# Second step of a long convolution: products taken from an SBUF copy of both halves, and one accumulator buffer for two quarters of the last step

## The chip, the cores and the metric

The kernel runs on one core of a Trainium2 chip. TensorE (PE) multiplies matrices into PSUM, an accumulator memory of eight banks; VectorE (DVE), ScalarE (ACT) and GpSimd (POOL) work elementwise; SyncE (SP) issues most of the DMAs. The metric is device time in microseconds (us) of one execution, as the median of several runs. Lower is better.

## The reference

Two branches over 2048 positions of 640 channels are mixed by a gate. Branch a is a long convolution whose filter comes from a state-space model of 128 modes per channel; branch b is a feed-forward network (FFN) with 1728 hidden units and a relu.

```python
g = sigmoid((x * gate_w).sum(-1, keepdims=True))        # x = A_u, [1, 2048, 640]
# branch a
dt = exp(log_dt); A = -exp(log_A_real) + 1j * A_imag; C = (C_real + 1j * C_imag) * dt[:, None]
P = exp((A * dt[:, None])[:, :, None] * arange(2048))   # [640, 128, 2048]
K = 2.0 * einsum("dn,dnl->dl", C, P).real
a = irfft(rfft(u^T, 4096) * rfft(K, 4096), 4096)[..., :2048]^T + u * D_skip
# branch b
b = maximum(x @ w1, 0) @ w2                             # w1 [640, 1728], w2 [1728, 640]
return g * a + (1 - g) * b
```

## The kernel before

**Three pieces of work.** `ssm` makes the filter K (up to about 404 us of the profile), `conv` convolves (from about 407 us to the end), `feed_forward` computes the FFN. The FFN's matmuls run all through the execution and take turns with the other two. Its 14 blocks of hidden units are handled in three parts (`PARTS`); partial sums of a part go to DRAM and come back for the next.

**The convolution.** `conv` takes the channels in five column groups of 128 (index `i`). A group passes through steps, each a set of small matmuls with an operation on another engine behind it:

- `stage1` (first step): four quarters of the filter and four of the signal are transformed; VectorE transposes the results into a buffer `ku` of 128 x 8 x 2 x 512, whose halves are called `K` and `U`. Two such buffers exist.
- `stage2` (second step): for each of eight indices `j`, TensorE writes 128 x 1024 results into one PSUM buffer `pc`: one half belongs to the filter, the other to the signal. Then they are multiplied as complex numbers: ScalarE copies the filter's half to `K`; VectorE makes two products of 128 x 512 (`mul(1)` first, into `U`, then `mul(0)`, into `K` in place), each reading the signal's half from PSUM and the filter's from SBUF; GpSimd combines them with one subtraction and one addition of 128 x 256 (`add`).
- `inv2` (next step): two halves `h` of four indices each. Each half takes two `pc` buffers, and ScalarE copies them back to `U` (128 x 1024 each). It needs the `add` results of its four indices.
- `relay`: eight VectorE transposes from `U` to `K`.
- `inv1` (last step): four quarters. TensorE writes 128 x 512 of a quarter into a `pc` buffer, of which half is used; ScalarE scales it by the gate in four instructions. Then the result is stored, or added to the FFN's sums and written out.

`pc` buffers come from a pool `psc` of three, each two PSUM banks. The FFN has two single banks of its own (`pf`). In the profile the second step's matmuls are `pc<-ku,tm`, those of `inv2` are `pc<-ku,tn`, those of `inv1` are `pc<-ku,tw`, and those of the first step are `pc<-ck,tf`, `pc<-cl,tf` and `pc<-xu,tf`.

**The order of the work.** No engine chooses at run time. A planner (`Plan.run`) lays out the whole kernel in advance: every operation is a task with an engine, a queue, an expected duration, its dependencies, a rank, and tokens of buffer rings (`take` when it begins to hold a buffer, `use` as long as it holds it). The instructions of an engine then stand in the order so found and wait for their operands by semaphores. FFN matmuls have rank 5, those of the second step and `inv2` rank 2, those of `inv1` rank 3. A task of VectorE marked `port` is planned longer when GpSimd is busy beside it:

```python
if t.port:                                                                     # L286
    self.free[e] += 0.25 * min(max(self.free['POOL'] - start, 0), t.dur)       # L288
```

The planner gives a product of the second step 0.62 us and each add 0.7 us. Most instructions are issued through one helper, so most rows of the profile carry its line, L314, and are told apart by the names of their tiles.

Of the kernel before, what the change touches and what calls it, by code (L numbers as in the profile page):

```python
# [10 lines left out]
F32 = mybir.dt.float32  # L11
# [14 lines left out]
S4R = 3  # L26
# [27 lines left out]
S2D = 1  # L54
# [5 lines left out]
PL = 2.5  # L60
YO = 5
YJ = 3
KRANK = 3
TN = 0.7

# [76 lines left out]
class Plan:  # L142
# [20 lines left out]
    def add(self, eng, q, dur, fn, deps=(), take=(), use=(), rank=5, mode=None, kb=0, port=False, n=0, late=False):  # L163
        t = Task()
        t.eng, t.q, t.dur, t.fn, t.deps, t.take, t.use, t.mode = eng, q, dur, fn, tuple(deps), take, use, mode
        t.prio, t.end, t.kb, t.lag, t.glue, t.port = rank + MOVES.get(self.n, 0), None, kb, self.LAG[eng], [], port
        t.n, t.late = n or dur / 0.13, late
        self.n += 1
        for b in (*take, *use):
            b.users += 1  # L170
            b.left += 1
        if q is not None:
            self.put(t, q)
        return t
# [170 lines left out]
class Kernel:  # L345
# [865 lines left out]
    def conv(self, C=128):  # L1211
        tc, nc, io, A, tok, ring = self.tc, self.nc, self.io, self.plan.add, self.plan.token, self.plan.ring
        V, S, P, D_ = self.V, self.S, self.P, self.D
        n, H = D // C, C // 2
        od = self.out.rearrange("(a h b) d -> h a b d", h=2, b=16)
        ud = io['A_u'][0].rearrange("(a b) d -> a b d", b=32)
        for k, v in dict(psc=3, ck=2, ckp=2, cu=1, yo=YO, yj=YJ, K=2).items():
            ring(k, v)
        st = {}

# [46 lines left out]
        K, first, pes = {}, {}, {}  # L1267
# [49 lines left out]
        def stage2(i, j, dep):  # L1317
            b_ = tok('psc')

            def pe():  # L1320
                ps = self.psc.tile([128, 2, 4, C], F32, name="pc")
                for a in range(2):
                    for m in range(4):
                        for p in range(2):
                            r, g = slice(p * 64, p * 64 + 64), 4 * j + m
                            x = st['ku', i].rearrange("p j k (e m t) -> p j m k e t", m=4, t=2)
                            self.E.matmul(ps[32 * m:32 * m + 32, p, 2 * a:2 * a + 2].rearrange("q k (e t) -> q k e t", t=2),
                                          st['tm'][r, g, 32 * a:32 * a + 32], x[r, j, m], start=True, stop=True)
                st['p2', i, j] = ps.rearrange("q p (a k) c -> q k a p c", a=2)

            def copy():
                S.copy(whole(i, j), st['p2', i, j][:, 0])

            def mul(a):
                def go():
                    k = whole(i, j)
                    V.tensor_mul(whole(i, j, 'U') if a else k, st['p2', i, j][:, 1, None, a].to_broadcast([128, 2, 2, C]), k)
                return go

            def add(k):  # L1340
                def go():
                    y, x = whole(i, j)[:, k], whole(i, j, 'U')[:, 1 - k]
                    (P.tensor_add if k else P.tensor_sub)(y, y, x)
                return go
            f = A('PE', None, 0.92, pe, dep, take=[b_], use=[K[i]], rank=S2P, mode='c', n=32)
            c = [A('ACT', 's2', 0.52, copy, [f], use=[b_, K[i]], rank=0.5)]
            for a in (1, 0):
                c.append(A('DVE', 's2', 0.62, mul(a), c, use=[b_, K[i]], rank=S2D))
            return f, [A('POOL', 's2', 0.7, add(k), c, use=[K[i]], rank=1) for k in range(2)]


        def whole(i, j, k='K'):
            return st[k, i][:, j].rearrange("q (b p c) -> q b p c", b=2, p=2)
# [40 lines left out]
        def inv1(i, j, dep):  # L1394
            last = i == n - 1
            for q in range(2):
                b_, b0 = tok('psc'), j * 8 + q * 4
                ns = min(max(2 * sum(c <= i for c in CG) - b0, 0), 4)
                y_ = tok('yo') if ns or not last else None
                g_, first = None, False  # L1400
                if last and ns < 4:
                    first = self.gy_tok is None
                    g_ = self.gy_tok = self.gy_tok or tok('K')

                def pe(q=q, b0=b0):
                    py = st['p4', i, b0] = self.psc.tile([128, 2, 4, C], F32, name="pc")
                    for h in range(2):
                        self.E.matmul(py[h * 64:h * 64 + 64, 0].rearrange("p b c -> p (b c)"), st['tw'],
                                      st['K', i][:, h * 4 + b0 // 4], start=True, stop=True)

                def copy(q=q, b0=b0, ns=ns, y_=y_, first=first):
                    if first:
                        self.gy = self.pr.tile([128, 8, 2, 512], F32, name="ku", bufs=2).rearrange("p j k (b c) -> p (j k b) c", c=C)
                    if y_:
                        st['yo', i, b0] = self.pr.tile([128, 4, C], F32, name="yo", bufs=YO)
                    x = st['p4', i, b0][:, 0].rearrange("p b c -> p (b c)").rearrange("p (c b) -> p b c", b=4)
                    for b in range(4):
                        o = self.gy[:, b0 + b] if last and b >= ns else st['yo', i, b0][:, b]
                        S.mul(o, x[:, b], self.gate[:, b0 + b:b0 + b + 1])
                a = A('PE', 's4', 0.87, pe, [*dep, tw], take=[b_], use=[K[i]], rank=S4R, mode='c1')  # L1420
                pes['4', i, b0] = a
                if JS4 and q:
                    self.plan.join([pes['4', i, b0 - 4], a])
                c = A('ACT', 's4', 1.24, copy, [a], take=[x for x in (y_, g_ if first else None) if x],
                      use=[b_] + ([g_] if g_ and not first else []), rank=S4A)
                self.need_gates.append(c)
                if ns < 4:
                    if not last:
                        def store(b0=b0, ns=ns):
                            stq.dma_start(self.sc['y'][:, b0 + ns:b0 + 4, i * C:i * C + C], st['yo', i, b0][:, ns:])  # L1430
                        c2 = A(STQ, 'y4', 0.62, store, [c], use=[y_], kb=64 * (4 - ns), rank=STR, late=True)
                    self.y_st[i, b0 // 4] = c if last else c2
                if ns:

                    new = not last or b0 == 0
                    if last:
                        j_ = self.yl_tok = tok('cu') if new else self.yl_tok
                    else:
                        j_ = tok('yj')

                    def load(b0=b0, ns=ns):
                        if last:
                            if b0 == 0:
                                st['yl'] = self.xu[:, :16 * C].rearrange(
                                    "p (b c) -> p b c", c=C)
                            st['yj', i, b0] = st['yl'][:, b0:b0 + 4]
                        else:
                            st['yj', i, b0] = self.pr.tile([128, 4, C], F32, name="yj", bufs=YJ)
                        for b in range(0, ns, 2):
                            D_.dma_start(st['yj', i, b0][:, b:b + 2],  # L1450
                                         self.sc['part'][(len(PARTS) - 1) % 2][(b0 + b) // 2][:, :, i * C:i * C + C])

                    def join(b0=b0, ns=ns):
                        y = st['yo', i, b0][:, :ns]
                        P.tensor_add(y, y, st['yj', i, b0][:, :ns])

                    def out(b0=b0, ns=ns):
                        for h in range(2):
                            stq.dma_start(od[h, :, b0:b0 + ns, i * C:i * C + C], st['yo', i, b0][64 * h:64 * h + 64, :ns])
                    ld = A('SP', 'yq', 0.62 * ((ns + 1) // 2), load, [opened], take=[j_] if new else (), use=() if new else [j_],  # L1460
                           kb=64 * ns, rank=3)
                    self.need_sums.append((ld, [(b0 + b) // 2 for b in range(0, ns, 2)]))
                    own = A('POOL', 's4', 0.1 + 0.3 * ns, join, [c, ld], use=[y_, j_], rank=2)
                    A(STQ, 'y4', 1.25, out, [own], use=[y_], kb=64 * ns, rank=STR, late=True)
# [4 lines left out]
        u = load_u(0)  # L1469
# [3 lines left out]
        dep = [x for q in range(4) for x in stage1('k', 0, q, lk[q])]  # L1473
# [67 lines left out]
```

## Time and profile before

| | before |
|---|---|
| median of 3 runs | 644.57 us (643.6 to 645.45) |
| the profiled execution, own time | 642.35 us |
| its span, first to last instruction | 640.6 us |
| TensorE busy | 617.3 us (96%) |
| VectorE busy | 508.5 us (79%) |
| ScalarE busy | 402.1 us (63%) |
| GpSimd busy | 93.9 us (15%) |
| granted TensorE clock | 1.0 |

The profile is one execution recorded by the hardware. A row names the engine, the operation, the tiles written and read, the shapes, how often it ran, its busy time in us and the mean of one in ns, and then how long its engine had been idle just before and what ended that idleness. A view by windows gives the busy time of each engine in stretches of the span. A timeline row has a start, a duration and the idle time before; neighbouring instructions of one kind are merged, with their count. Matmuls overlap, so the duration of one is longer than the distance to the next.

### The profile page before, as it was taken

What the parts mean: (1) busy time and instruction counts of PE and PEld (TensorE: products, weight loads), DVE (VectorE), ACT (ScalarE), POOL (GpSimd) and SP (SyncE); (2) the same over time, 40 slices, a digit from 0 to 9 for tenths busy, and PEclk for the clock granted to TensorE, in tenths of its full rate; (3) what the DMA queues carried; (4) which work ended last, traced back from release to release, by engine and by line L of the source; (5) the groups of instructions that cost most, each with busy time, mean ns of one, the idle gap of its engine ahead of it and who ended that gap; (6) DMA issues with size and microseconds to landing.
All of it is one profiled execution on the core that took longest, in us unless ns stands there. A gap on an engine that the chain in (4) does not pass through costs nothing.

```text
span 640.6 us, 19212 instructions
## 1 busy us (share of the span) xinstructions
PE 617.3 (96%) x8236; PEld 503.0 (79%) x8236; DVE 508.5 (79%) x818; ACT 402.1 (63%) x603; POOL 93.9 (15%) x134
## 2 busy tenths in 40 slices
PE   7989999899999899999999999999999999999897
PEld 6989998798898798898898898665565556756577
DVE  4889936989999999998999999768579753966542
ACT  5557439999999988988978985113443424432550
POOL 0000000000000000000000000024151531713633
PEclk9999999999999999999999999999999999999999
DMA  9974774333456734373454225794406558156355
GB/s 256 326 236 147 221 229 165 105 125 112 136 167 210 255 122 144 122 242 117 129 198 154 79 80 176 258 315 132 144 3 215 185 164 263 53 158 188 102 166 133
DMA packets 76176, 107.78 MB, mean 168 GB/s; under 512 B 7610, under 2 KB 58682, under 8 KB 75195
## 3 DMA queue, kind: packets, MB, share of 16 engines
q1 hardware_dynamic: 75930, 106.14, 53.2%
q8 instruction: 65, 1.06, 0.7%
q10 hardware_dynamic: 160, 0.41, 0.3%
q14 instruction: 21, 0.16, 0.1%
HBM read 67.47 MB, written 44.30 MB: 174 GB/s over the span
## 4 chain that ended last, share of the span: by engine, by line
PE 56%; DVE 5%; DMA 2%; ACT 2%; issue 1%; SPq 1%; DVEq 0%; ACTq 0%
PE pf L314 35%; PE pc L314 13%; PE pk L314 4%; DVE ku L314 3%; PE pg L314 2%; PE px L314 2%; DMA part<-q 1%; ACT ku L314 1%; PE pe L314 1%; DMA out_dram<-yo 1%; SPq L314 1%; DVE sn L314 1%; ACT cs L314 0%; DVE q L314 0%; ACT q L314 0%
## 5 line engine op out<-in xcount | busy, mean ns | idle before, releaser
L314 PE MATMUL pf<-xx,w1h 128*128 128x256 f32 (+1 forms) x760 | 184.2, 339 | 0.4 <-DVE xx L314 0.3
L314 PEld LDWEIGHTS pf<-xx,w1h 128*128 128x128 f32 x760 | 125.2, 189 | 22.8 <-issue 7.3
L314 PE MATMUL pf<-xx,w1l 128*128 128x512 f32 (+1 forms) x340 | 115.7, 340 | 0.0
L314 PE MATMUL pf<-w2h,hh 128*128 128x320 f32 x288 | 89.7, 315 | 2.4 <-DVE hl L314 1.5
L314 PE MATMUL pf<-w2l,hh 128*128 128x320 f32 x288 | 87.8, 309 | 0.0
L314 ACT COPY ku<-pc 128x512 f32<-128x512 f32 (+1 forms) x60 | 43.8, 761 | 68.2 <-PE pc L314 56.7
L314 PE MATMUL pf<-w2h,hl 128*128 128x320 f32 x256 | 73.3, 312 | 0.0
L314 PEld LDWEIGHTS pf<-xx,w1l 128*128 128x128 f32 x340 | 64.3, 189 | 7.6 <-DVE w1l L314 0.2
L314 POOL TENSOR_TENSOR kt<-kt,dsk 128x8 f32<-128x8 f32 x20 | 10.3, 515 | 392.7 <-DVE kt L314 377.8
L314 POOL TENSOR_TENSOR ku<-ku 128x256 f32<-128x256 f32 x80 | 56.2, 737 | 55.3 <-DVE ku L314 49.1
L314 DVE TENSOR_TENSOR ku<-pc,ku 128x512 f32<-128x512 f32 x80 | 52.6, 684 | 12.5 <-ACT ku L314 11.3
L314 DVE STREAM_TRANSPOSE ku<-pc 128x512 f32<-128x512 f32 x80 | 50.2, 683 | 13.7 <-PE pc L314 13.7
L314 PEld LDWEIGHTS pf<-w2h,hh 128*128 128x128 f32 x288 | 54.1, 188 | 7.7 <-issue 3.7
L314 DVE TENSOR_TENSOR sn<-pg,cs 128x1024 f32<-128x1024 f32 x40 | 48.7, 1217 | 7.5 <-ACT cs L314 7.5
L314 PEld LDWEIGHTS pf<-w2l,hh 128*128 128x128 f32 x288 | 54.1, 188 | 0.6
L314 ACT ACT_TABLE_LOAD x42 | 53.9, 1283 | 0.7
L314 ACT CAST cs<-pg 128x1024 int32<-128x1024 f32 x40 | 40.3, 1008 | 21.2 <-PE pg L314 21.0
L314 DVE TENSOR_TENSOR mg<-mg,cs 128x1024 f32<-128x1024 f32 x40 | 48.9, 1222 | 1.3
L314 PEld LDWEIGHTS pf<-w2h,hl 128*128 128x128 f32 x256 | 46.4, 188 | 3.5 <-issue 2.9
L314 PE MATMUL pc<-ku,tm 64*32 64x256 f32 x1280 | 42.2, 392 | 3.6 <-DVE ku L314 2.4
L314 ACT ACTIVATE cs<-cs,half_pi 128x1024 f32<-128x1024 f32 x40 | 45.6, 1140 | 0.0
L314 ACT ACTIVATE hh<-pf 128x512 fp32r<-128x512 f32 (+1 forms) x40 | 20.5, 513 | 39.4 <-PE pf L314 39.4
(170 smaller groups left out, 1232.5 us busy)
## 6 DMA issues: line engine op xcount, KB each, us to landing
xx<-xt SPq DMA_DIRECT2D x24, 640.0 KB, 6.8
xt<-xx SPq DMA_DIRECT2D x16, 640.0 KB, 3.9
part<-q SPq DMA_DIRECT2D x16, 640.0 KB, 3.4
q<-part SPq DMA_DIRECT2D x16, 640.0 KB, 5.3
ws<-in_B_w_dram SPq DMA_DIRECT2D x20, 320.0 KB, 5.5
kd<-kt SPq DMA_DIRECT2D x80, 64.0 KB, 1.8
ub<-in_A_u_dram SPq DMA_DIRECT2D x10, 512.0 KB, 4.7
xu<-ub SPq DMA_DIRECT2D x5, 1024.0 KB, 6.2
```

Source lines behind the costliest of these rows:

```text
L314: self._last = self._tc.keep_in_program_order(f(*a, **k))
```

## The change

All eight indices `j` of the second step are handled in a new way (`FULL`). ScalarE copies both halves of the PSUM buffer, 128 x 1024, to `K` and `U`. The two products read the signal's half from `U` in place of PSUM; `mul(1)` writes into a new SBUF buffer `ut` (two of them, `UT`), and the adds read it from there. In the planner the PSUM buffer's token is no longer held by the products, the products are marked `port`, and the copy is given 0.96 us in place of 0.52. In the last step the two quarters `q` of one `j` use the two halves of one `pc` buffer, in place of a buffer each.

```diff
+FULL = tuple(range(8))
+UT = 2
+FULLR = 0
...
-        for k, v in dict(psc=3, ck=2, ckp=2, cu=1, yo=YO, yj=YJ, K=2).items():
+        for k, v in dict(psc=3, ck=2, ckp=2, cu=1, yo=YO, yj=YJ, K=2, ut=UT).items():
...
+            full = j in FULL
+            t_ = tok('ut') if full else None
+
             def copy():
-                S.copy(whole(i, j), st['p2', i, j][:, 0])
+                if full:
+                    S.copy(st['ku', i][:, j].rearrange("q k (a p c) -> q k a p c", a=2, p=2), st['p2', i, j])
+                else:
+                    S.copy(whole(i, j), st['p2', i, j][:, 0])
 
             def mul(a):
                 def go():
                     k = whole(i, j)
-                    V.tensor_mul(whole(i, j, 'U') if a else k, st['p2', i, j][:, 1, None, a].to_broadcast([128, 2, 2, C]), k)
+                    u = whole(i, j, 'U')[:, a] if full else st['p2', i, j][:, 1, a]
+                    if a:
+                        st['x2', i, j] = whole(i, j, 'U')
+                        if full:
+                            st['x2', i, j] = self.pr.tile([128, 4 * C], F32, name="ut", bufs=UT).rearrange("q (b p c) -> q b p c", b=2, p=2)
+                    V.tensor_mul(st['x2', i, j] if a else k, u[:, None].to_broadcast([128, 2, 2, C]), k)
                 return go
 
             def add(k):
                 def go():
-                    y, x = whole(i, j)[:, k], whole(i, j, 'U')[:, 1 - k]
+                    y, x = whole(i, j)[:, k], st['x2', i, j][:, 1 - k]
                     (P.tensor_add if k else P.tensor_sub)(y, y, x)
                 return go
             f = A('PE', None, 0.92, pe, dep, take=[b_], use=[K[i]], rank=S2P, mode='c', n=32)
-            c = [A('ACT', 's2', 0.52, copy, [f], use=[b_, K[i]], rank=0.5)]
+            c = [A('ACT', 's2', 0.96 if full else 0.52, copy, [f], use=[b_, K[i]], rank=0.5)]
             for a in (1, 0):
-                c.append(A('DVE', 's2', 0.62, mul(a), c, use=[b_, K[i]], rank=S2D))
-            return f, [A('POOL', 's2', 0.7, add(k), c, use=[K[i]], rank=1) for k in range(2)]
+                c.append(A('DVE', 's2', 0.62, mul(a), c, take=[t_] if full and a else (), use=[K[i]] + ([] if full else [b_]), rank=S2D + FULLR * full,
+                           port=full))
+            return f, [A('POOL', 's2', 0.7, add(k), c, use=[K[i]] + ([t_] if full else []), rank=1) for k in range(2)]
...
             for q in range(2):
-                b_, b0 = tok('psc'), j * 8 + q * 4
+                b0 = j * 8 + q * 4
+                b_ = b_ if q else tok('psc')
...
-                    py = st['p4', i, b0] = self.psc.tile([128, 2, 4, C], F32, name="pc")
+                    if not q:
+                        st['p4', i, j] = self.psc.tile([128, 2, 4, C], F32, name="pc")
+                    py = st['p4', i, j]
                     for h in range(2):
-                        self.E.matmul(py[h * 64:h * 64 + 64, 0].rearrange("p b c -> p (b c)"), st['tw'],
+                        self.E.matmul(py[h * 64:h * 64 + 64, q].rearrange("p b c -> p (b c)"), st['tw'],
...
-                a = A('PE', 's4', 0.87, pe, [*dep, tw], take=[b_], use=[K[i]], rank=S4R, mode='c1')
+                a = A('PE', 's4', 0.87, pe, [*dep, tw], take=() if q else [b_], use=[K[i]] + ([b_] if q else []), rank=S4R, mode='c1')
```

More of the change, by code (lines that the diff above doesn't have):

```diff
@@ L1403, in inv1, with pe, copy @@
                     g_ = self.gy_tok = self.gy_tok or tok('K')
-                def pe(q=q, b0=b0):
-                    py = st['p4', i, b0] = self.psc.tile([128, 2, 4, C], F32, name="pc")
+                def pe(q=q, b0=b0, j=j):
+                    if not q:
+                        st['p4', i, j] = self.psc.tile([128, 2, 4, C], F32, name="pc")
+                    py = st['p4', i, j]
                     for h in range(2):
-                        self.E.matmul(py[h * 64:h * 64 + 64, 0].rearrange("p b c -> p (b c)"), st['tw'],
+                        self.E.matmul(py[h * 64:h * 64 + 64, q].rearrange("p b c -> p (b c)"), st['tw'],
                                       st['K', i][:, h * 4 + b0 // 4], start=True, stop=True)
-                def copy(q=q, b0=b0, ns=ns, y_=y_, first=first):
+                def copy(q=q, b0=b0, ns=ns, y_=y_, first=first, j=j):
                     if first:
@@ L1415, in copy @@
                         st['yo', i, b0] = self.pr.tile([128, 4, C], F32, name="yo", bufs=YO)
-                    x = st['p4', i, b0][:, 0].rearrange("p b c -> p (b c)").rearrange("p (c b) -> p b c", b=4)
+                    x = st['p4', i, j][:, q].rearrange("p b c -> p (b c)").rearrange("p (c b) -> p b c", b=4)
                     for b in range(4):
```

## The prediction

> **What bounds the kernel now.** I read first the page's busy shares, then the same count for the stretch from 400 us on, where all the edited code runs, and then what TensorE waited for there.
>
> ```profile
> span 640.6 us, 19212 instructions
> PE 617.3 (96%) x8236; PEld 503.0 (79%) x8236; DVE 508.5 (79%) x818; ACT 402.1 (63%) x603; POOL 93.9 (15%) x134
> ```
> ```profile
> 400.00:640.60 240.60, 231.84 (x3677) 150.96 (x3675) 154.07 (x251) 83.50 (x168) 82.98 (x108) 1.00 0.55 166
> ```
> ```profile
> PE pc L314 <- DVE ku L314: 3.1, 6, 1.7
> PE pc L314 <- ACT ku L314: 1.0, 1, 1.0
> ```
>
> The columns of the second fence are PE, PEld, DVE, ACT and POOL. TensorE is busy for 231.84 of the last 240.60 us at full clock. Only 8.76 us are open, and its waits for the convolution's own engines are 4.1 us of them. So no gain here can be large; a loss can, because TensorE's order is fixed beforehand and a late operand stops everything behind it.
>
> The second look is at the five stretches in which the second step runs, one per column group, from about its first copy to its last add:
>
> ```profile
> 426.30:440.80 14.50, 14.33 (x373) 9.72 (x362) 12.45 (x20) 4.70 (x8) 11.27 (x16) 1.00 0.59 178
> 460.30:474.50 14.20, 14.08 (x328) 9.29 (x315) 13.93 (x23) 5.01 (x9) 11.25 (x16) 1.00 0.01 3
> 501.20:515.60 14.40, 14.09 (x264) 8.90 (x249) 12.03 (x19) 4.81 (x9) 11.30 (x17) 1.00 0.51 150
> 543.50:558.70 15.20, 15.17 (x359) 10.43 (x352) 14.89 (x24) 6.96 (x12) 12.75 (x18) 1.00 0.18 56
> 592.50:602.40 9.90, 7.30 (x87) 3.91 (x86) 7.45 (x12) 5.79 (x15) 9.88 (x15) 1.00 0.28 69
> sum 68.20, PE 64.97 PEld 42.24 DVE 60.74 ACT 27.26 POOL 56.45; mean PE 12.99 PEld 8.45 DVE 12.15 ACT 5.45 POOL 11.29
> ```
>
> Here VectorE (12.15 us of a mean 13.64) and GpSimd (11.29) are both nearly full. They fit into 13.64 us only because they run at the same time. This is what the change touches.
>
> **The change part by part.** The prices of the operations:
>
> ```profile
> L314 POOL TENSOR_TENSOR ku<-ku 128x256 f32<-128x256 f32 x80 | 56.2, 737 | 55.3 <-DVE ku L314 49.1 <-PE pf L314 6.2
> L314 DVE TENSOR_TENSOR ku<-pc,ku 128x512 f32<-128x512 f32 x80 | 52.6, 684 | 12.5 <-ACT ku L314 11.3
> L314 DVE TENSOR_TENSOR cs<-me,cs 128x512 f32<-128x512 f32 x40 | 27.3, 682 | 0.0
> L314 ACT COPY ku<-pc 128x512 f32<-128x512 f32 x40 | 23.3, 593 | 42.7 <-PE pc L314 42.7
> L314 ACT COPY ku<-pc 128x1024 f32<-128x1024 f32 x20 | 20.7, 1095 | 25.5 <-PE pc L314 14.0 <-issue 11.5
> ```
>
> *The copy.* It grows from 128x512 (593 ns) to 128x1024 (1095 ns): 0.50 us, times 40 is 20 us more ScalarE work. ScalarE has 157 us open after 400 us, so this is free but for the first copy of each stage, which makes the stage 0.5 us later. FFN matmuls hide that; uncovered it would be 5 x 0.5 = 2.5 us. What queues behind it is FFN evictions and the next step's copies, each up to 0.5 us later; the two FFN banks cover this.
>
> *The buffer.* It comes free after the copy, not after two products. That ends the 3.1 us of waits for DVE (bounds 0 and the 4.1 us of both rows); I take 3.1. It also lets the eight matmul groups of a stage run in fewer bursts. What a change of pattern costs:
>
> ```profile
> 544.60 0.73 PE L314 MATMUL pf<-xx,w1h 128*128 128x512 f32 x2
> 545.40 0.62 PE L314 MATMUL pf<-xx,w1h 128*128 128x512 f32 x2
> 546.09 0.61 PE L314 MATMUL pf<-xx,w1h 128*128 128x512 f32 x2
> 546.54 0.39 PE L314 MATMUL pf<-xx,w1l 128*128 128x512 f32 x1
> 546.86 3.26 PE L314 MATMUL pc<-ku,tm 64*32 64x256 f32 x96
> ```
>
> Nine FFN matmuls take 2.26 us (544.60 to 546.86). The middle three took 0.69 (545.40 to 546.09), so 2.07 would do: some 0.2 us per round trip. The second step comes in 18 bursts in TensorE's timeline, of which these are the first and the last:
>
> ```profile
> 425.06 2.99 PE L314 MATMUL pc<-ku,tm 64*32 64x256 f32 x96
> ...
> 596.37 1.16 PE L314 MATMUL pc<-ku,tm 64*32 64x256 f32 x32 [0.50 <-DVE ku L314]
> ```
>
> With two bursts per stage it would be 10, so 8 fewer.
>
> *The shared buffer of the last step.* Its two quarters go into the two halves of one buffer, four quarters into two buffers. Now the last one or two of the four come apart from the others in four of the five stages, for want of a third or fourth buffer; I take 3 round trips less. If the second quarter's matmuls had to wait for the first quarter's four copies, it would cost up to 1.2 us ten times; different halves give no reason for that, so zero. Together 11 round trips x 0.2 = 2.2. Gain: 3.1 + 2.2 = **5.3 us**.
>
> *The products.* They now read two SBUF operands. Alone that costs nothing: 682 ns for the SBUF form, 684 for the present one. [...]
>
> *Products against adds.* GpSimd's adds read two SBUF operands too. The trace of before has such a meeting only in the filter stage, where GpSimd adds 128x8:
>
> ```profile
> L314 POOL TENSOR_TENSOR kt<-kt,dsk x20: 209/568/572, 121.0 to 404.2; 128x8 f32<-128x8 f32 x20
> ```
> ```profile
> 138.51 0.65 DVE L314 SCALAR_TENSOR_TENSOR G<-mg,sn 128x512 f32<-128x512 f32 x1
> 139.09 0.69 DVE L314 TENSOR_TENSOR G<-mg,sn 128x512 f32<-128x512 f32 x1
> ```
> ```profile
> 138.67 0.57 POOL L314 TENSOR_TENSOR kt<-kt,dsk 128x8 f32<-128x8 f32 x1 [17.42 <-DVE kt L314]
> 404.23 0.21 POOL L314 TENSOR_TENSOR kt<-kt,dsk 128x8 f32<-128x8 f32 x1 [11.11 <-DVE kt L314]
> ```
>
> The add takes 0.21 us when VectorE is idle and 0.57 when it meets a VectorE instruction with two SBUF operands: it ends at 139.24, 0.08 after that instruction (139.16). GpSimd waited for its end, though 0.13 of its own 0.21 ran underneath. The present products meet the adds without that: the 80 adds lie within 721 and 757 ns. How far a product waits for an add no row shows. Bounds per group of two products and two adds: 1.4 (GpSimd's two adds, as now) and 2 x 0.65 + 2 x 0.70 = 2.7 us. I take strict alternation with 0.13 hidden at each of four turns, 2.7 - 0.52 = 2.2 us, as the kt row has it. [...]
>
> *What that does to TensorE.* The order is laid out with the products stretched by a quarter of the overlap (line 288), about 1.55 us a group. At 2.2, the eight groups end 8 x 0.65 = 5.2 us later than the order allows for. The next step's second half then waits, less the slack that stands there now:
>
> ```profile
> 439.31 1.42 POOL L314 TENSOR_TENSOR ku<-ku 128x256 f32<-128x256 f32 x2 [0.21 <-DVE ku L314]
> 471.62 2.82 POOL L314 TENSOR_TENSOR ku<-ku 128x256 f32<-128x256 f32 x4 [0.95 <-PE pf L314]
> 507.18 8.36 POOL L314 TENSOR_TENSOR ku<-ku 128x256 f32<-128x256 f32 x12 [0.21 <-DVE ku L314]
> 557.24 1.44 POOL L314 TENSOR_TENSOR ku<-ku 128x256 f32<-128x256 f32 x2 [0.38 <-DVE ku L314]
> 591.28 11.11 POOL L314 TENSOR_TENSOR ku<-ku 128x256 f32<-128x256 f32 x16
> ```
> ```profile
> 453.58 2.09 PE L314 MATMUL pc<-ku,tn 32*64 32x128 f32 x128
> 476.44 2.10 PE L314 MATMUL pc<-ku,tn 32*64 32x128 f32 x128
> 539.20 2.09 PE L314 MATMUL pc<-ku,tn 32*64 32x128 f32 x128
> 560.23 2.09 PE L314 MATMUL pc<-ku,tn 32*64 32x128 f32 x128
> 608.92 2.09 PE L314 MATMUL pc<-ku,tn 32*64 32x128 f32 x128
> ```
>
> Slack is 2.0 us in the second stage (474.44 to 476.44), 1.55 in the fourth, 6.5 in the last; in the first and third it is over 12. So TensorE stands 3.2 + 3.65 = 6.9 us. Queued behind the held products on VectorE are FFN evictions, two or three a stage; TensorE has one other bank of 12 matmuls to go on with,
>
> ```profile
> 623.67 13.12 PE pf L314 x88
> ```
>
> 12 x 13.12 / 88 = 1.8 us. An eviction at the stage's end is 5.2 - 1.8 = 3.4 us too late, one in its first third not at all; the mean over the places in it is 3.4 x 3.4 / (2 x 5.2) = 1.1 a stage, 5.5 for five (bounds 0 and 17). Loss: 6.9 + 5.5 = **12.4 us**.
>
> **Sum.** The profiled execution took 642.35 us (the span, and 1.75 around it). 642.35 - 5.3 + 12.4 = 649.45. The median of the runs is 2.2 above that execution, so I forecast **651.7 us**.
>
> **The rivals.**
> *Faster: the collision is covered.* If GpSimd alone waits, in gaps that VectorE leaves anyway, the groups end within the order's 1.55 us, nothing of the 12.4 us appears, and the 5.3 us are gained: 642.35 - 5.3 + 2.2 = 639. For it: all products could run ahead, as buffers no longer hold them; against it: 12.15 of 13.64 us leave VectorE few gaps. It decides below 1.55 + 2/8 = 1.8 us a group.
> *Full exclusion, 2.7 us a group.* The lag is 8 x 1.15 = 9.2 us; the next step waits 7.2 + 7.65 + 2.7 = 17.5, evictions cost 7.4 x 7.4 / (2 x 9.2) = 3.0 a stage, 15 for five: 32.5 - 5.3 = +27, so 672 us. For it: the kt add did wait out its instruction; against it: 0.13 of it ran underneath.
> *No net change.* Burst gains and a lag of some 2 us each in the two tight stages cancel: 644.6. So too if something else holds the buffer, such as the matmuls of the next column group taking it at once until their transposes are done: no gain without a loss.
>
> **How the numbers follow.** A measurement of this kernel can tell about 0.3%, 1.9 us, from no change. Forecast case (646 to 662) 0.48, full exclusion (662 to 680) 0.13, faster (635 to 642.5) 0.33, no change 0.06. So slower 0.61, same 0.06, faster 0.33. Signs are mixed, so the likeliest case's own range is 646 to 662. The range 638 to 668 leaves out the best of the faster case (its other end, with all 4.1 us of waits gone and more bursts merged) and the worse half of full exclusion, under 2 in 10.
>
> **What would show it.** Right, if: the 128x256 adds rise well above 737 ns or the new products above 684; the copies are 40 of 128x1024 near 1.1 us; the second step's matmuls come in some ten bursts; TensorE has new waits, for GpSimd before the 32x64 matmuls and for VectorE before FFN ones; the stages grow from 13.6 towards 19 us. Wrong, if adds and products keep their durations, or if they stretch and TensorE's waits do not grow, because the order put other work there. A PE sum that changes by more than 3 us would mean that bursts, not waits, decide.

## The result, and the profile after

The changed kernel takes 664.09 us (median of 6 runs, 661.64 to 665.02) against 643.56 us (median of 6) for the kernel before: a ratio of 1.0316, 95% interval 1.0299 to 1.0334. It is 20.5 us slower. The forecast was 651.7, slower by 7.1: the right side, inside the range, and the size wrong by a factor of nearly three.

The page of the changed kernel, the stretch from 400 us to its end (columns as before), and what TensorE waited for in the whole span:

```profile
span 662.0 us, 19231 instructions
PE 622.5 (94%) x8236; PEld 514.7 (78%) x8236; DVE 531.7 (80%) x818; ACT 415.9 (63%) x603; POOL 115.4 (17%) x134
```
```profile
400.00:662.00 262.00, 236.34 (x3676) 162.06 (x3674) 177.32 (x251) 97.36 (x168) 104.44 (x108) 0.97 0.50 151
```
```profile
PE pf L317 <- DVE q L317: 14.5, 5, 3.8
...
PE pf L317 <- DVE w2l L317: 1.8, 2, 1.2
...
PE pc L317 <- DVE ku L317: 0.7, 2, 0.5
...
PE pc L317 <- POOL ku L317: 0.2, 1, 0.2
```

The 21.4 us of longer span are two things. TensorE stands 25.7 us in this stretch (262.00 - 236.34) where it stood 8.76: 16.9 more. And the same matmuls keep it busy for 236.34 us where they took 231.84: 4.5 more, at a granted clock of 0.97. The waits for a buffer held by products (DVE ku) are nearly gone, 0.7 of 3.1 us. In their place it waits for FFN evictions on VectorE, 14.5 us in five waits.

The five stages of the second step, from first copy to last add:

```profile
426.20:447.10 20.90, 16.32 (x281) 11.32 (x266) 17.83 (x21) 9.07 (x10) 15.33 (x16) 0.93 0.52 152
466.60:489.50 22.90, 19.29 (x437) 14.19 (x444) 19.71 (x25) 12.21 (x13) 15.66 (x16) 0.98 0.27 87
514.30:536.30 22.00, 17.43 (x275) 10.91 (x254) 18.92 (x22) 11.23 (x19) 17.05 (x18) 0.92 0.47 131
556.20:579.10 22.90, 19.48 (x436) 15.73 (x435) 19.86 (x27) 12.10 (x14) 17.09 (x18) 0.96 0.32 97
603.60:625.20 21.60, 18.67 (x421) 13.36 (x409) 16.62 (x19) 12.23 (x18) 16.63 (x17) 0.92 0.28 74
```

They last 22.1 us in the mean, where they lasted 13.6. The groups of instructions show why (from 404 us on):

```profile
L317 ACT COPY ku<-pc 128x1024 f32<-128x1024 f32 x60 | 58.2, 1063 | 59.1 <-PE pc L317 59.0
L317 POOL TENSOR_TENSOR ku<-ku,ut 128x256 f32<-128x256 f32 x80 | 77.4, 995 | 65.5 <-DVE ku L317 39.0 <-ACT ku L317 24.7 <-ACT yo L317 1.8
L317 DVE TENSOR_TENSOR ku<-ku 128x512 f32<-128x512 f32 x40 | 40.3, 1006 | 4.0 <-PE pc L317 0.5
L317 DVE TENSOR_TENSOR ut<-ku 128x512 f32<-128x512 f32 x40 | 37.3, 932 | 12.3 <-ACT ku L317 6.6 <-POOL ku L317 3.1 <-DMA ck<-kd 2.5
```

An add takes 995 ns in the mean (737 before), the two products 932 and 1006 (684 before). The timelines of VectorE and of GpSimd in the first stage show the turns that they take:

```profile
435.89 1.20 DVE L317 TENSOR_TENSOR ut<-ku 128x512 f32<-128x512 f32 x1 [0.62 <-ACT ku L317]
437.19 1.03 DVE L317 TENSOR_TENSOR ku<-ku 128x512 f32<-128x512 f32 x1
438.15 0.68 DVE L317 TENSOR_TENSOR ut<-ku 128x512 f32<-128x512 f32 x1
438.93 1.05 DVE L317 TENSOR_TENSOR ku<-ku 128x512 f32<-128x512 f32 x1
```
```profile
433.67 4.01 POOL L317 TENSOR_TENSOR ku<-ku,ut 128x256 f32<-128x256 f32 x4 [0.69 <-DVE ku L317]
438.37 4.02 POOL L317 TENSOR_TENSOR ku<-ku,ut 128x256 f32<-128x256 f32 x4 [0.69 <-DVE ku L317]
```

GpSimd starts a pair of groups every 4.70 us (433.67 to 438.37), 2.35 us a group. A product that begins while GpSimd is idle still takes 0.68 us (at 438.15), and the add behind it is held; products that begin while an add runs take 1.03 to 1.20. Not all of the pace is this exclusion: five times `ut<-ku` waits for the adds to release one of the two `ut` buffers, 3.1 us in all (POOL ku in its row). Whether more such buffers would quicken the turns was not tried.

The second step's matmuls now come in long bursts, 256 in a row in the fourth stage,

```profile
556.75 7.68 PE L317 MATMUL pc<-ku,tm 64*32 64x256 f32 x256
```

and in TensorE's timeline I count 7 bursts for the 18 before.

### The profile page after: what moved, and what is told of

Read it like the earlier page. It is cut to its first block, busy times and chain, and to the rows that moved or that the text cites. A ratio compares the mean times of both kernels' runs of the same rounds, so it can differ in the third digit from the quotient of the medians.

```text
span 662.0 us, 19231 instructions
## 1 busy us (share of the span) xinstructions
PE 622.5 (94%) x8236; PEld 514.7 (78%) x8236; DVE 531.7 (80%) x818; ACT 415.9 (63%) x603; POOL 115.4 (17%) x134
## 4 chain that ended last, share of the span: by engine, by line
PE 45%; DVE 7%; DMA 4%; issue 4%; ACT 2%; SPq 2%; POOL 2%; DVEq 0%; ACTq 0%; POOLq 0%
PE pf L317 28%; PE pc L317 9%; PE pk L317 4%; DVE ut L317 3%; SPq L317 2%; DVE ku L317 2%; POOL ku L317 2%; PE pg L317 2%; PE px L317 2%; DMA part<-q 1%; DMA out_dram<-yo 1%; PE pe L317 1%; DMA y__84<-yo 1%; ACT ku L317 1%; DVE q L317 1%
## 5 line engine op out<-in xcount | busy, mean ns | idle before, releaser
L317 PE MATMUL pf<-w2h,hh 128*128 128x320 f32 x288 | 91.2, 321 | 16.9 <-DVE q L317 14.5
L317 ACT COPY ku<-pc 128x1024 f32<-128x1024 f32 x60 | 58.2, 1063 | 59.1 <-PE pc L317 59.0
L317 POOL TENSOR_TENSOR ku<-ku,ut 128x256 f32<-128x256 f32 x80 | 77.4, 995 | 65.5 <-DVE ku L317 39.0
L317 ACT ACTIVATE hh<-pf 128x512 fp32r<-128x512 f32 (+1 forms) x40 | 20.5, 511 | 57.3 <-PE pf L317 57.3
L317 DVE TENSOR_TENSOR ut<-ku 128x512 f32<-128x512 f32 x40 | 37.3, 932 | 12.3 <-ACT ku L317 6.6
L317 DVE TENSOR_TENSOR ku<-ku 128x512 f32<-128x512 f32 x40 | 40.3, 1006 | 4.0 <-PE pc L317 0.5
```

The source lines that it names most:

```text
L317: self._last = self._tc.keep_in_program_order(f(*a, **k))
```

## The experiments

The theory to be tested: products with two SBUF operands and adds exclude each other; VectorE falls behind its fixed order; what stands behind the products on VectorE comes late, and TensorE stands. The rivals: the new order of the work is itself worse, or ScalarE's longer copies are. Each run is compared with runs of the kernel before on the same chip; their medians were 642.28 us (small adds, the long copy, the old order, the planner that knows), 642.72 (the control to the small adds, GpSimd only writes, adds on VectorE, the shared buffer alone) and 643.18 (both kernels with evictions moved, quarters unshared, only group 0).

**Small adds.** The changed kernel, its adds cut to 128x8:

```diff
+                    y, x = y[:, :, :4], x[:, :, :4]
                     (P.tensor_add if k else P.tensor_sub)(y, y, x)
```

> The changed kernel with its order instruction for instruction as it is, but each add of the second step does only 128x8 of its 128x256 elements (the rest of the additions is left out). Collision theory (the products with two SBUF operands and the adds exclude each other, VectorE falls behind, FFN evictions come late, TensorE stands): the products return to about 0.69 us, TensorE's 14.5 us of waits for DVE q fall under 3, its clock stays at 1.0, time 637 to 645 us. Order theory (the new order of the work is itself worse): 657 us or more. Copy theory (ScalarE's longer copies hold others up): 657 us or more.

638.41 us, ratio 0.9941 (0.9919 to 0.9962). Its TensorE instructions stand in the same order as in the changed kernel. So the order is no loss, nor is the longer copy in it: both are still there, and the kernel is faster than before. The products are back at 692 and 721 ns, and no wait for sums (DVE q) is left. Even a 128x8 add meets the products:

```profile
429.04 0.68 POOL L317 TENSOR_TENSOR ku<-ku,ut 128x8 f32<-128x8 f32 x2 [24.66 <-DVE ku L317]
...
437.96 0.36 POOL L317 TENSOR_TENSOR ku<-ku,ut 128x8 f32<-128x8 f32 x2 [1.57 <-DVE ku L317]
```

Two of them take 0.68 us beside a product and 0.36 beside an eviction, which reads one of its operands from PSUM.

**Its control: small adds in the kernel before**, by the same line.

> Control to the small adds: the kernel before, its order unchanged, each add of the second step doing 128x8 of its 128x256 elements (the rest of the additions is left out). Collision theory: the adds of the kernel before collide with nothing and only lengthen a chain that FFN matmuls cover, so 640 to 644 us. If shorter adds are worth something by themselves, 639 us or less, and the gain of the small adds in the changed kernel is partly that.

643.23 us, ratio 0.9995 (0.997 to 1.002). Shorter adds are worth nothing by themselves.

**GpSimd only writes.** The changed kernel, each add replaced by a memset that keeps GpSimd busy without a read:

```diff
-                    (P.tensor_add if k else P.tensor_sub)(y, y, x)
+                    y = whole(i, j)
+                    P.memset(y, 0.0)
```

> The changed kernel in its own order, but each add is replaced by a GpSimd memset of 128x512, which writes SBUF and reads nothing (the additions are left out). If products and adds meet where both read: products 0.69 us, 637 to 643 us, as with the small adds. If GpSimd's writing excludes VectorE as well: products 0.85 us or more, and 648 us or more.

638.38 us, ratio 0.9924 (0.9898 to 0.9951). Its stretch from 400 us, and its products and memsets:

```profile
400.00:636.10 236.10, 227.06 (x3675) 153.84 (x3673) 155.65 (x251) 97.70 (x168) 69.20 (x108) 1.00 0.56 167
```
```profile
L317 POOL MEMSET ku<- 128x512 f32 x80 | 42.1, 527 | 73.1 <-DVE ku L317 45.6 <-ACT ku L317 25.2
L317 DVE TENSOR_TENSOR ku<-ku 128x512 f32<-128x512 f32 x40 | 28.8, 719 | 3.7
L317 DVE TENSOR_TENSOR ut<-ku 128x512 f32<-128x512 f32 x40 | 28.1, 702 | 10.8 <-ACT ku L317 8.3 <-DMA ck<-kd 2.5
```

GpSimd works 42.1 us, much of it beside VectorE: from 432 to 436 us it is busy for 2.95 us and VectorE for 3.69 of the 4.00, so they overlap for at least 2.64. The products take 702 and 719 ns. So GpSimd's writing does not hold them; the adds, which read two SBUF operands, do (932 and 1006 ns in the changed kernel). TensorE's order is again that of the changed kernel, so this pair tells the loss apart without a change of order: 9.0 us of standing against 25.7 (16.6 more), and 227.06 us busy against 236.34 (9.3 more) for the same instructions.

**The changed second step in the old order.** The kernel before, its planner untouched:

```diff
-                S.copy(whole(i, j), st['p2', i, j][:, 0])
+                S.copy(st['ku', i][:, j].rearrange("q k (a p c) -> q k a p c", a=2, p=2), st['p2', i, j])
...
+                    if a:
+                        st['x2', i, j] = self.pr.tile([128, 4 * C], F32, name="ut", bufs=2).rearrange("q (b p c) -> q b p c", b=2, p=2)
-                    V.tensor_mul(whole(i, j, 'U') if a else k, st['p2', i, j][:, 1, None, a].to_broadcast([128, 2, 2, C]), k)
+                    V.tensor_mul(st['x2', i, j] if a else k, whole(i, j, 'U')[:, a][:, None].to_broadcast([128, 2, 2, C]), k)
```

> The kernel before in its own order of instructions, with the changed kernel's second step: copy of both halves, products from two SBUF operands into the new buffers, adds from there. The last step keeps its separate buffers. Collision theory: adds near 1.0 us and products near 0.95 as in the changed kernel, stages near 21 us, and as this order allows nothing for it, at least the changed kernel's loss: 660 to 675 us. Order theory: 643 to 648 us, since the order is the old one. Copy theory: like the long copy alone, 655 us or more.

676.06 us, ratio 1.0516 (1.0462 to 1.057), the slowest of all and just above the range. Adds take 988 ns, products 892 and 970, near those of the changed kernel. The collision costs more where the order knows nothing of it, though the longer copy, priced next, is part of this loss.

```profile
PE pf L314 <- DVE q L314: 7.8, 4, 5.5
PE pf L314 <- DVE w1l L314: 5.2, 1, 5.2
PE pc L314 <- issue: 4.7, 1, 4.7
PE pc L314 <- ACT ku L314: 4.0, 5, 2.0
```

Most of this time is for what stands behind products on VectorE: sums, and the low parts of the hidden units.

**The long copy alone**, in the old order: only the first of the edits just shown (the copy of both halves).

> The kernel before in its own order; only ScalarE's copy takes both halves, 128x1024 in place of 128x512; the products still read the signal's half from PSUM. Collision theory: the copy is covered, at most 0.5 us a stage, 643 to 647 us. Copy theory: most of the 20 us of the change, 655 us or more. Order theory: no change, 643 to 645 us.

647.46 us, ratio 1.008 (1.006 to 1.010). It costs 5.2 us there, a little more than the collision theory had it and far less than the copy theory. TensorE waits for buffers that are now held half a microsecond longer, 7.1 us in place of 4.1:

```profile
PE pc L314 <- DVE ku L314: 4.6, 6, 1.9
PE pc L314 <- ACT ku L314: 2.5, 7, 1.3
```

In the profiled execution the granted clock was also lower, 0.993 in the mean, with 8 tenths in two of the page's 40 slices (210.2 to 226.3 and 598.2 to 614.4 us), which may be part of the rest. In the changed kernel's order the copy is covered, as the two fast kernels above show.

**A planner that knows.** The changed kernel with durations near those of its own profile in the plan:

```diff
-                c.append(A('DVE', 's2', 0.62, mul(a), c, ... port=full))
+                c.append(A('DVE', 's2', 0.95, mul(a), c, ... port=False))
-            return f, [A('POOL', 's2', 0.7, add(k), ...
+            return f, [A('POOL', 's2', 1.05, add(k), ...
```

> The changed kernel, but the planner is told what the profile after shows: a product 0.95 us in place of 0.62, an add 1.05 in place of 0.7 (and no stretch for overlap on top). The instructions are the same, only their order can differ. If the loss is that the order did not know of the collision: evictions move ahead of products, TensorE's waits for DVE q fall to 5 us or less, 645 to 653 us. If VectorE simply has too much to do in the stages: 657 us or more.

653.84 us, ratio 1.0175 (1.0145 to 1.0204), just above the 653 expected. Of the 20.5 us, 11.6 are left. So nearly half of the loss, 9 us, is that the order did not know: the waits for sums fall from 14.5 us to those of this row.

```profile
PE pf L317 <- DVE q L317: 2.9, 4, 1.6
```

The rest stays. Adds of 963 ns and products of 849 and 914 say that the two engines still take turns here; that this is what is left of the loss is argued, not shown.

**Adds on VectorE.** Nothing on GpSimd beside the products:

```diff
-                    (P.tensor_add if k else P.tensor_sub)(y, y, x)
+                    (V.tensor_add if k else V.tensor_sub)(y, y, x)
...
-                           port=full))
+                           port=False))
-            return f, [A('POOL', 's2', 0.7, add(k), ...
+            return f, [A('DVE', 's2', 0.36, add(k), ...
```

> The changed kernel with the adds on VectorE in place of GpSimd (planned at 0.36 us each, products without a stretch). Nothing runs on GpSimd beside the products, so no collision; VectorE then has some 2 x 0.65 + 2 x 0.4 = 2.1 us a group in place of the 2.36 us of products and adds in turns. Collision theory: products 0.69 us, TensorE's clock near 1.0, 643 to 652 us. Theory that two SBUF operands are slow by themselves or that the burst order is the loss: 657 us or more.

659.91 us, ratio 1.0267 (1.0225 to 1.0308): a miss, above the 652 expected. The products are free of the collision, as expected:

```profile
427.32 0.69 DVE L317 TENSOR_TENSOR ut<-ku 128x512 f32<-128x512 f32 x1 [2.48 <-DMA xx<-xt]
428.11 0.69 DVE L317 TENSOR_TENSOR ku<-ku 128x512 f32<-128x512 f32 x1
428.84 0.76 DVE L317 TENSOR_TENSOR ku<-ku,ut 128x256 f32<-128x256 f32 x2
429.52 0.68 DVE L317 TENSOR_TENSOR ut<-ku 128x512 f32<-128x512 f32 x1
```

But a group takes VectorE 2.20 us (427.32 to 429.52), hardly less than the 2.35 of the turns, and the time is hardly less either. TensorE waits 8.6 us for DVE ku and 5.6 for sums, and the granted clock is 0.991. This fits a reading by which it counts what a stage costs VectorE's queue, not whether it works or is held; as the order was laid out anew, the run does not show that by itself.

**Evictions off VectorE.** The changed kernel; ScalarE scales the last part's sums into place:

```diff
-                    V.scalar_tensor_tensor(st['q', g][:, t, ns], ps, self.omg[:, b:b + 1], st['q', g][:, t, ns],
-                                           op0=ALU.mult, op1=ALU.add)
+                    S.mul(st['q', g][:, t, ns], ps, self.omg[:, b:b + 1])
```

> The changed kernel in its own order, but the last part's FFN evictions leave VectorE's queue: ScalarE scales the sums into place (the addition of the earlier sum is left out); TensorE's order is unchanged. If the loss reaches TensorE by evictions that stand behind held products: the waits for DVE q (14.5 us) are gone, the clock no longer falls, 645 to 652 us, the rest being waits for the next step. If it reaches TensorE by the adds themselves (the next step's operands): 658 us or more, the waits move to the 32x64 matmuls.

656.51 us, ratio 1.0201 (1.0163 to 1.0238), between the two expectations. The waits for sums are gone, and 13.3 of the 20.5 us are left. Against what was expected, the clock still falls (0.986 over the profile), for other waits have taken their place:

```profile
PE pc L317 <- issue: 4.8, 2, 4.3
PE pc L317 <- DVE ku L317: 4.1, 1, 4.1
PE pc L317 <- POOL ku L317: 3.6, 11, 0.6
```

The 4.1 us are first-step matmuls that wait for a buffer whose transposes now stand behind the products. The 4.3 us come before the same matmuls of a later column group; the profile names no releaser for them. So the evictions are one door among several through which the same lag reaches TensorE.

**Its control**, the same move in the kernel before.

> Control: the same move of the last part's evictions in the kernel before (the addition is left out). By either theory TensorE does not wait for those evictions there, so 641 to 645 us.

643.26 us, ratio 1.0001 (0.9984 to 1.0018): nothing, as expected.

**The parts of the change.** First the shared buffer without the new second step (`FULL = ()`):

> The changed kernel with no index in the new way (FULL empty): the second step as before, only the last step's quarters share a buffer; the planner lays out its order anew. Collision theory: nothing collides, 640 to 645 us. Order theory (the shared buffer's order is the loss): 655 us or more.

645.14 us, ratio 1.0051 (1.0026 to 1.0076), at the edge of what was expected: it brings nothing, and the kernel is about 2 us slower in its new order. Then the new second step without the shared buffer (a `tok('psc')` and a tile for each quarter, as before):

> The changed kernel without its second edit: each quarter of the last step has its own buffer again. Collision theory: the collision is all there, 655 to 668 us. If the shared buffer is a large part of the loss: 652 us or less.

663.98 us, ratio 1.0321 (1.0284 to 1.0358): the whole loss. Last, only group 0 of each stage in the new way, quarters unshared (`FULL = (0,)`):

> Only the first group of each stage in the new way (FULL holds index 0), quarters with their own buffers. Its products run before any add of the stage, so they meet none on GpSimd; its PSUM buffer comes free early. Collision theory: no product above 0.75 us, 641 to 645 us. If new-way products cost in any place: a fifth to an eighth of the loss, 646 us or more.

647.36 us, ratio 1.0056 (1.0026 to 1.0085), by its time nearer to the second expectation. But its products meet no add. The five in place take 693 ns in the mean, and the answer for the tile `ut` shows the others (min, median, max in ns):

```profile
L317 DVE TENSOR_TENSOR ut<-ku x5: 648/691/693, 427.2 to 582.7; 128x512 f32<-128x512 f32 x5
```

What its 4 us are is open. Its runs spread from 643.4 to 651.1 us and go in the main with the granted clock: the two at 1.000 took 643.39 and 643.61, the two at 0.988 and 0.989 took 651.06 and 649.08. So falls of the clock may be much of it; no run separates them. No version tried beats the kernel before with the full computation.

## Why the prediction was right or wrong

**Right.** The products' price without adds (682 ns forecast, 702 and 719 beside memsets). The collision, and about its pace: 2.2 us a group forecast from a row of 128x8 adds, 2.35 measured. The agreement is partly luck: in the first stage VectorE also stands some 0.62 us in every second group, for a `ut` buffer or a copy, and the sum has no such wait. The exclusion is seen here in both directions, which the trace of before could not show for VectorE: products go from 0.68 to 1.20 us, adds from 737 to 995 ns. Full exclusion, with the one that comes second held for the whole instruction, is not borne out: by the prediction's bound that would be 2.7 us a group, against 2.35. Memsets on GpSimd, which only write, did not contend: products of 702 and 719 ns.

**Right by luck: the gain without the collision**, 5.3 us forecast and 4.3 measured (642.72 to 638.38, the memset kernel). The sum had 3.1 us from waits and 2.2 from bursts. In the memset kernel the waits for DVE ku are gone, but TensorE stands 9.0 us where it stood 8.76, as other waits have come (ACT yo 2.2 us). The whole gain is in busy time, 227.06 us for 231.84, more than twice the term for bursts. By the prediction's own sign, a PE sum that moves by more than 3 us, it is bursts and not waits that decide here; no run varies the bursts alone.

**Slightly off.** The copy was taken as covered, 2.5 us at worst. In the changed kernel's order it is; alone in the old order the kernel is 5.2 slower. The shared buffer was to bring some 0.6 us and brought none. Bursts fell from 18 to 7, more than the 10 forecast.

**Wrong: the step "What that does to TensorE", 12.4 us in place of 26.** Compared with the memset kernel, which has the same order, the loss is 25.9 us of span (636.1 to 662.0), and it has two terms: one mis-sized, one put at nothing.

The first is standing, 16.6 us against 12.4, and its parts were put in the wrong place. The next step was to wait 6.9 us; it waits 0.2 (POOL ku). This is not for want of a lag: in the memset kernel, the new order leaves less slack there than the old one (0.2, 0.4 and 1.4 us in the second, fourth and fifth stage, where the prediction read 2.0, 1.55 and 6.5). TensorE meets the lag earlier, at FFN tiles that stand in front of the next step and whose bank waits for an eviction behind held products. In the second stage it resumes at 488.02 and comes to the next step at 489.31, about when the last adds end (489.46):

```profile
488.02 0.41 PE L317 MATMUL pf<-w2h,hh 128*128 128x320 f32 x1 [2.41 <-DVE q L317]
489.31 3.31 PE L317 MATMUL pc<-ku,tn 32*64 32x128 f32 x128
```

The evictions were to cost 5.5; they cost 14.5, and the low parts of the hidden units 1.8 more. I had averaged over the places of an eviction in the stage. In the new order the one that TensorE waits for stands late: behind the last products in two stages, behind those of the seventh of eight groups in two, and of the fifth in one.

The second is the clock, for which the sum had no term at all. TensorE's timeline behind the first long wait, and its windows of 1 us (the granted clock is the third column from the right):

```profile
443.45 0.42 PE L317 MATMUL pf<-w2h,hh 128*128 128x320 f32 x1 [2.96 <-DVE q L317]
443.70 0.31 PE L317 MATMUL pf<-w2l,hh 128*128 128x320 f32 x1
443.85 0.31 PE L317 MATMUL pf<-w2h,hl 128*128 128x320 f32 x1
...
444.72 0.47 PE L317 MATMUL pf<-w2h,w1h 128*128 128x320 f32 x1
444.98 0.47 PE L317 MATMUL pf<-w2l,w1h 128*128 128x320 f32 x1
```
```profile
443.00:444.00 1.00, 0.55 (x4) 0.55 (x5) 1.00 (x2) 0.00 (x0) 0.92 (x2) 1.00 0.11 46
445.00:446.00 1.00, 1.00 (x5) 1.00 (x5) 1.00 (x3) 0.65 (x1) 0.36 (x1) 0.50 0.14 51
```

Some 0.6 us after TensorE resumes here, the clock falls to 0.50 for some 3.4 us, and matmuls follow each other at 0.26 us in place of 0.15. Added up over windows of 4 us (what the clock is short of 1.00, times the window), the clock lacks 8.6 us in the changed kernel, in five such falls of 1.7 us, one at each wait for sums; in the memset kernel each such window from 400 to 632 us shows 1.00. That is most of the 9.3 us by which the same matmuls are busy longer.

In the sum's own terms, by the spans: -4.5 for the order and the buffers (640.6 to 636.1), 16.6 for standing, 9.3 for busy time, together the 21.4 by which the spans differ. The rival of full exclusion, 672 us, had the size more nearly, but by a wrong pace (2.7) and with the same missing term.

## What to carry to other kernels

Before products are moved from PSUM to SBUF operands, ask what GpSimd reads at that time: two engines that fitted side by side into 13.6 us a stage took turns, and the stage lasted 22.1. A fixed order passes such a lag on through whatever stands behind the held instructions, so price it at the end of the stage and not in its mean, in the new order and not by the slacks of the old. Where TensorE is the bound, a wait can cost more than itself: here each of five, of 2.40 to 3.75 us, brought 1.7 us of slower matmuls on top.

## What the runs showed of the hardware

The prediction had no fall of the clock. In the changed kernel the waits with which it fell were of 2.40, 2.41, 2.93, 2.96 and 3.75 us. Length alone does not decide. The 14th of a page's 40 slices, some 16 us long, has a clock of 8 tenths in the pages of five kernels here and of 9 (90% or more) in those of eight. With a wait of 2.1 us in it, before the matmuls `pg<-tg,PS`, the clock of the kernel before (first row) is 1.00 from 215 to 216 us; the long copy alone (second row) has the 8 tenths in its slice from 210.2 to 226.3 us:

```profile
213.73 0.73 PE L314 MATMUL pg<-tg,PS 128*128 128x512 f32 x2 [2.11 <-DVE sn L314]
```
```profile
213.82 0.73 PE L314 MATMUL pg<-tg,PS 128*128 128x512 f32 x2 [2.11 <-DVE sn L314]
```

Where a fall begins can be worked out from windows of 0.5 us (a clock of 0.58 from 444.00 to 444.50 is 0.08 us at 1.00 and the rest at 0.50). In the changed kernel the five begin at 444.08, 488.45, 532.82, 577.20 and 618.16 us, from 1.3 us after TensorE resumes to 0.4 before. By the same count each lasts 3.41 or 3.42 us. They lie 44.37, 44.37, 44.38 and 40.96 us apart, which is 13, 13, 13 and 12 times 3.413. So in this profile the falls fit a beat of about their own length; that it matters how a wait lies in it is my reading, and no run varies that alone.

The exclusion of VectorE and GpSimd showed where both read two SBUF operands: two adds of 128x8 were held for 0.3 us by one product (0.68 us against 0.36). Memsets of 527 ns, which read nothing, ran beside products of 702 and 719 ns, and adds beside products that read one operand from PSUM kept their 737 ns.
